# Attention with unshifted exponentials, units of 256 queries, three pairs of score banks and an instruction order from a simulation

## The chip, the cores and the metric

The kernel runs on one core of one Trainium2 chip. The metric is the time of one execution on the device, in microseconds (us). Engines are named as in the profile: PE is the matrix engine (PEld its weight loads), ACT the scalar engine, DVE the vector engine, POOL the GpSimd engine, SP the engine that issues the DMAs. "The granted clock" is the profile's record of how much of its full speed PE was allowed, 1.00 being all of it.

For one core a run counts as slow when it is over 1.5% longer than the fastest run of the same kernel on that occasion.

## The reference

Two attention layers without common data, joined along the last axis. Each has 2048 tokens, width 1024 and 32 heads of 32 columns. The inputs are bfloat16.

```python
# A: ordinary attention, all 2048 x 2048 scores of every head
qkv = (x @ wqkv).reshape(B, S, 3, H, Dh) ...
scores = einsum('bhqd,bhkd->bhqk', q, k) * Dh ** (-0.5)
o = einsum('bhqk,bhkd->bhqd', softmax(scores), v)
a = o... @ wo

# B: four segments of 512 tokens, causal within a segment, with a memory M, z
phi = lambda t: where(t > 0, t + 1.0, exp(t))
for s in range(4):
    p = softmax(qs @ ks.T * scale + causal_mask)
    a_dot = p @ vs
    a_mem = (phi(qs) @ M) / (phi(qs) @ z + 1e-06)
    outs.append(g * a_mem + (1.0 - g) * a_dot)      # g = sigmoid(beta), per head
    M = M + phi(ks).T @ vs
    z = z + phi(ks).sum()
b = concat(outs) @ wo
return concatenate([a, b], axis=-1)
```

The work that can't be avoided is the exponentials of the scores: 134 million in A, and about 21 million in B with some padding. They all go through ACT.

## The kernel before

A Python builder makes the program. It records operations one after the other, keeps a rough clock for each engine, and at each step of PE's clock picks what PE does next: scores first, then the product of probabilities and values (PV), then projections. What comes out is a fixed queue of instructions for each engine, with semaphores between the queues. The order of each queue is fixed when the program is built.

Work comes in units of four heads and 512 queries: 32 of A (16 tiles of 128 keys) and 32 of B, taken in turn. Of the eight PSUM banks that the program uses, two pairs hold scores, two single banks serve the projections and all other side work, one holds the PV sums and one the softmax denominators.

The scores of two heads go into one pair of banks, and one exponential of 128x1024 takes them out. It subtracts a shift, which it reads as one number per partition (`bias=cb`):

```python
SLOTS = [(0, 1), (2, 3)]
PROJ = [4, 5]
OB, LB = 6, 7
# ... emit_scores: n = 2 heads at a time, one bank for each
        for part in range(npart):
            for bk, (st, h) in zip(banks, todo):
                # ...
                    mms.append((self.ps[:, bk, off:off + w], lhsT, rhs))     # 32 rows x 512 queries
        # ...
        cb = (self.cbA if u.kind == "A" else self.cbB)[b][:, 0:1]
        op = R.op("ACT", lambda e: e.activation(self.PT[:, s0:s0 + n, 0:width], self.ps[:, banks[0]:banks[0] + n, 0:width],
                                                ACTF.Exp, bias=cb, scale=SCALE),
                  r=[("ps", bk) for bk in banks[:n]] + [("cb" + u.kind, b)], w=[("PT", s0 + i) for i in range(n)], ...)
```

The shift is an upper bound of the scores, from the largest norms of keys and queries. Each unit of B makes its own, and each group of heads of A. It is a serial chain over four engines:

```python
# b_prep, after the projections of keys and queries of this unit
        for k in range(2):
            R.op("DVE", ... tensor_tensor(self.SQB[k], KQ[:, k, :], KQ[:, k, :], ALU.mult))       # squares
        R.op("PE", ... matmul(self.ps[32 * r:32 * r + 32, bank, :], self.blk32, self.SQB[r % 2]))  # sums per head
        op = R.op("DVE", ... tensor_reduce(self.cbB[b][:, 1:2], self.ps[:, bank, :], AX.X, ALU.max))
        R.op("POOL", ... partition_all_reduce(self.cbB[b][:, 1:2], ..., bass_isa.ReduceOp.max))
        R.op("POOL", ... tensor_scalar(self.cbB[b][:, 0:1], self.cbB[b][:, 1:2], -SCALE, None, ALU.mult))
```

The denominators come out of PE repeated over 32 partitions, and all 128x512 of them go through DVE's reciprocal, in four pieces:

```python
# finish
        for q in range(4):
            cs = slice(128 * q, 128 * q + 128)
            R.op("DVE", lambda e, cs=cs: e.reciprocal(Ls[:, cs], Ls[:, cs]), ..., cost=0.9)
```

The input x of both layers is transposed on the way in by DMA: eight transposes of 128 columns by 2048 rows for A, with B's first unit and its loads issued ahead of them. Projections are full matmuls of 128x128 against 512 columns; V is projected with x as the weights.

## Time and profile before

Two executions took 1605.93 and 1631.54 us, median 1618.74. The profile is of an execution with a span of 1628.9 us.

| | before |
|---|---|
| PE busy | 1393.8 us, 86% |
| ACT busy | 1239.1 us, 76% |
| DVE busy | 792.3 us, 49% |
| mean granted clock | 0.905 |

These lines are from the page of the kernel before: busy time, share of the span and number of instructions of each engine, two lines of the table of 40 slices (busy tenths, and granted clock in tenths), and three groups (busy us in all, mean ns of one, then the idle time of the engine just before them and what ended it).

```profile
span 1628.9 us, 26663 instructions
...
PE 1393.8 (86%) x11550; PEld 466.4 (29%) x11696; DVE 792.3 (49%) x1196; ACT 1239.1 (76%) x1250; POOL 151.8 (9%) x344
...
ACT  0228999698789973969769996478888995598970
...
PEclk9997999798589999979669999688989999998999
...
L392 ACT ACTIVATE PT<-ps,cbA 128x1024 bf16<-128x1024 f32 x1024 | 1050.0, 1197 | 112.9 <-PE ps L380 112.1
L380 PE MATMUL ps<-QA,KA 32*128 32x512 bf16 x2048 | 421.6, 410 | 40.3 <-ACT PT L392 15.3
...
L464 DVE RECIPROCAL Ls<-Ls 128x128 f32<-128x128 f32 x256 | 242.2, 946 | 3.6
```

No engine is full over the whole span. ACT is at nine or ten tenths in some slices and at three to seven in others, and the clock sags in most of the same places.

The waits of the kernel before (who waited for whom: us in all, times, longest):

```profile
ACT PT L392 <- PE ps L380: 145.8, 136, 30.6
ACT PT L392 <- POOL cbB L615: 87.8, 12, 14.2
ACT E L631 <- DVE KQB L508: 55.0, 6, 18.3
...
POOL cbB L615 <- issue: 225.1, 32, 7.6
```

ACT waits for scores, for the shift of B's units, and for B's projections. The last line is inside POOL: after each of the 32 all-reduces of B the next POOL instruction starts about 7 us later (225.1 / 32), though the record of the all-reduce itself is only 0.38 us long. So each shift takes at least 7 us on POOL alone.

The table by stretches (busy us of each engine with the number of instructions, then granted clock, DMA share, GB/s):

```profile
0.00:110.00 110.00, 53.41 (x399) 24.78 (x404) 31.12 (x59) 8.26 (x10) 8.97 (x29) 0.97 0.47 106
110.00:1579.00 1469.00, 1297.74 (x10963) 423.96 (x11098) 739.14 (x1105) 1230.80 (x1240) 142.85 (x315) 0.90 0.11 27
1579.00:1629.00 50.00, 42.62 (x194) 17.61 (x196) 22.04 (x32) 0.00 (x0) 0.00 (x0) 1.00 0.19 69
...
410.00:420.00 10.00, 10.00 (x68) 3.04 (x66) 4.55 (x6) 7.23 (x8) 0.00 (x0) 0.50 0.00 0
```

The fourth number in each row after the length is ACT. Subtracting it from the length gives ACT's idle time: 102 us at the start, 238 in the middle, 50 at the end. The last row is in one of the bouts at half clock: PE busy for all of 10 us, and ACT, which waits for it, for 7.23.

The timeline of the kernel before (start, length, what, how many in a row without a gap), first of ACT, then two lines of PE:

```profile
67.62 2.91 ACT L392 ACTIVATE PT<-ps,cbB 128x1024 bf16<-128x1024 f32 x3 [14.22 <-POOL cbB L615]
...
230.34 31.41 ACT L392 ACTIVATE PT<-ps,cbA 128x1024 bf16<-128x1024 f32 x31
261.37 0.90 ACT L631 ACTIVATE E<-KQB 128x512 bf16<-128x512 bf16 x1
...
413.84 1.11 ACT L392 ACTIVATE PT<-ps,cbA 128x1024 bf16<-128x1024 f32 x1 [0.40 <-PE ps L380]
415.36 1.11 ACT L392 ACTIVATE PT<-ps,cbA 128x1024 bf16<-128x1024 f32 x1 [0.40 <-PE ps L380]
...
1570.61 0.39 PE L380 MATMUL ps<-QA,KA 32*128 32x512 bf16 x2
1570.93 0.40 PE L444 MATMUL ps<-PT,VA 128*32 128x512 bf16 x4
1571.15 0.39 PE L444 MATMUL ps<-PT,ones 128*32 128x512 bf16 x4
```

The first exponential is at 67.62 us, after a wait for the shift. Where nothing disturbs ACT, 31 exponentials start between 230.34 and 261.37 us, so the pitch, start to start, is 1.001 us; at half clock it is 1.52 us (415.36 - 413.84), because PE then takes as long to deliver scores. One visit to the scores, two matmuls of 32 rows by 512 columns, holds PE for 0.32 us (1570.93 - 1570.61). Without a change of tiling, a round of 512 columns takes 0.22 us (1571.15 - 1570.93, four matmuls side by side).

### The profile page before, as it was taken

What the parts mean: (1) busy time and instruction counts of PE and PEld (TensorE: products, weight loads), DVE (VectorE), ACT (ScalarE), POOL (GpSimd) and SP (SyncE); (2) the same over time, 40 slices, a digit from 0 to 9 for tenths busy, and PEclk for the clock granted to TensorE, in tenths of its full rate; (3) what the DMA queues carried; (4) which work ended last, traced back from release to release, by engine and by line L of the source; (5) the groups of instructions that cost most, each with busy time, mean ns of one, the idle gap of its engine ahead of it and who ended that gap; (6) DMA issues with size and microseconds to landing.
All of it is one profiled execution on the core that took longest, in us unless ns stands there. A gap on an engine that the chain in (4) does not pass through costs nothing.

```text
span 1628.9 us, 26663 instructions
## 1 busy us (share of the span) xinstructions
PE 1393.8 (86%) x11550; PEld 466.4 (29%) x11696; DVE 792.3 (49%) x1196; ACT 1239.1 (76%) x1250; POOL 151.8 (9%) x344
## 2 busy tenths in 40 slices
PE   1588999698999987969889998879898997789998
PEld 0241233223223233322223323222332232222223
DVE  0343444353255654645526754545545745463643
ACT  0228999698789973969769996478888995598970
POOL 0000001001011010100101100100101101110100
PEclk9997999798589999979669999688989999998999
DMA  8220001002011001100111101100111001310002
GB/s 167 84 47 7 14 22 39 21 14 46 14 33 27 20 21 46 27 14 21 40 27 28 26 21 27 40 13 20 30 37 33 21 1 27 97 27 7 20 30 75
DMA packets 166742, 54.17 MB, mean 33 GB/s; under 512 B 160480, under 2 KB 160480, under 8 KB 166624
## 3 DMA queue, kind: packets, MB, share of 16 engines
q1 hardware_dynamic: 166624, 52.45, 13.2%
q8 instruction: 92, 1.51, 0.4%
q14 instruction: 26, 0.21, 0.0%
HBM read 35.65 MB, written 8.39 MB: 27 GB/s over the span
## 4 chain that ended last, share of the span: by engine, by line
ACT 57%; PE 23%; issue 8%; DVE 6%; SPq 3%; DMA 2%; POOL 1%; POOLq 0%; ACTq 0%; DVEq 0%
ACT PT L392 56%; PE ps L380 6%; PE ps L444 6%; PE ps L505 5%; PE ps L710 4%; PE ps L522 3%; DVE Ls L464 2%; SPq L293 1%; SPq L306 1%; DMA beta<-in_B_beta_dram 1%; DVE outsb L717 1%; DVE Ls L454 1%; DMA out_dram<-outsb 1%; ACT E L631 1%; DVE cbB L610 1%
## 5 line engine op out<-in xcount | busy, mean ns | idle before, releaser
L392 ACT ACTIVATE PT<-ps,cbA 128x1024 bf16<-128x1024 f32 x1024 | 1050.0, 1197 | 112.9 <-PE ps L380 112.1
L380 PE MATMUL ps<-QA,KA 32*128 32x512 bf16 x2048 | 421.6, 410 | 40.3 <-ACT PT L392 15.3
L392 ACT ACTIVATE PT<-ps,cbB 128x768 bf16<-128x768 f32 (+1 forms) x192 | 175.3, 1039 | 121.7 <-POOL cbB L615 87.8
L444 PE MATMUL ps<-PT,ones 128*32 128x512 bf16 (+3 forms) x2560 | 256.0, 395 | 0.0
L464 DVE RECIPROCAL Ls<-Ls 128x128 f32<-128x128 f32 x256 | 242.2, 946 | 3.6
L380 PEld LDWEIGHTS ps<-QA,KA 32*128 32x128 bf16 x2048 | 96.9, 92 | 462.7 <-ACT PT L392 399.0
L444 PE MATMUL ps<-PT,VA 128*32 128x512 bf16 x2048 | 216.4, 413 | 0.9 <-DVE Os L455 0.4
L505 PE MATMUL ps<-xB,WB 128*128 128x512 bf16 x472 | 147.7, 417 | 53.6 <-DMA xB<-in_B_x_dram 18.2
L505 PE MATMUL ps<-xA,WA 128*128 128x512 bf16 x459 | 141.7, 405 | 29.5 <-DMA xA<-in_A_x_dram 18.9
L415 POOL TENSOR_SCALAR_AFFINE_SELECT PT<-PT 128x256 bf16<-128x256 bf16 (+1 forms) x192 | 95.2, 498 | 472.1 <-ACT PT L392 469.2
L380 PE MATMUL ps<-KQB 32*128 32x128 bf16 (+3 forms) x512 | 65.9, 335 | 50.6 <-ACT PT L392 48.2
L454 DVE COPY Ls<-ps 128x512 f32<-128x512 f32 x64 | 44.0, 687 | 107.4 <-PE ps L444 106.8
L508 DVE CAST KQB<-ps 128x512 bf16<-128x512 f32 x64 | 43.6, 681 | 102.1 <-PE ps L505 102.1
L527 DVE CAST VA<-ps 128x512 bf16<-128x512 f32 x32 | 21.8, 682 | 146.5 <-PE ps L522 146.5
L657 DVE RECIPROCAL den<-den 128x128 f32<-128x128 f32 x96 | 91.3, 951 | 2.5
L444 PEld LDWEIGHTS ps<-PT,VA 128*32 128x32 bf16 x2048 | 53.0, 93 | 129.5 <-issue 120.8
L717 DVE CAST outsb<-ps 128x512 bf16<-128x512 f32 x64 | 43.5, 685 | 84.1 <-PE ps L710 72.0
L522 PE MATMUL ps<-WA,xA 128*128 128x128 bf16 x1024 | 82.5, 231 | 0.8 <-DVE VA L527 0.8
L522 PE MATMUL ps<-WB,xB 128*128 128x128 bf16 x1024 | 79.1, 230 | 1.7 <-DVE KA L508 0.5
L444 PE MATMUL ps<-PT,VB 128*32 128x256 bf16 (+3 forms) x512 | 45.9, 356 | 35.6 <-POOL PT L415 34.6
L710 PE MATMUL ps<-WoB,OTB 128*128 128x512 bf16 x237 | 68.3, 403 | 7.8 <-DVE PKt L678 2.6
L505 PEld LDWEIGHTS ps<-xB,WB 128*128 128x128 bf16 x512 | 40.8, 101 | 107.8 <-issue 67.2
(70 smaller groups left out, 900.1 us busy)
## 6 DMA issues: line engine op xcount, KB each, us to landing
WB<-in_B_wk_dram SPq DMA_DIRECT2D x32, 256.0 KB, 2.9
WB<-in_B_wq_dram SPq DMA_DIRECT2D x32, 256.0 KB, 2.9
WB<-in_B_wv_dram SPq DMA_DIRECT2D x32, 256.0 KB, 2.9
out_dram<-outsb SPq DMA_DIRECT2D x32, 256.0 KB, 2.0
WA<-in_A_wqkv_dram SPq DMA_DIRECT2D x24, 256.0 KB, 2.9
WoB<-in_B_wo_dram SPq DMA_DIRECT2D x1, 2048.0 KB, 17.6
xA<-in_A_wo_dram SPq DMA_DIRECT2D x1, 2048.0 KB, 9.5
xB<-in_B_x_dram SPq DMA_TRANSPOSE x32, 2.8
```

The costliest lines, as they stand in the source:

```text
L380: ins = e.matmul(o, l, r, start=True, stop=True)
L392: op = R.op("ACT", lambda e: e.activation(self.PT[:, s0:s0 + n, 0:width], self.ps[:, banks[0]:banks[0] + n, 0:width], ACTF.Exp, bias=cb, s ...
L415: mo = R.op("POOL", lambda e, ap=ap, pat=pat: e.affine_select(ap, ap, pattern=pat, compare_op=ALU.is_ge, fill=0.0, base=0, channel_multipl ...
L444: ins = e.matmul(o, l, r, start=(st == 0), stop=stop)
L454: R.op("DVE", lambda e: e.tensor_copy(self.Ls2[x][:, :], self.ps[:, LB, :]), r=[("ps", LB)], w=[("Ls", x)], cost=0.66)
L464: R.op("DVE", lambda e, cs=cs: e.reciprocal(Ls[:, cs], Ls[:, cs]), r=[("Ls", x)], w=[("Ls", x)], cost=0.9)
L505: ins = e.matmul(self.ps[:, bank, :], W[:, i, :], xsl(i), start=(i == 0), stop=(i == NI - 1))
L508: op = R.op("DVE", lambda e: e.tensor_copy(dst, self.ps[:, bank, :]), r=[("ps", bank)], w=[dkey], cost=0.66)
L522: ins = e.matmul(self.ps[:, bank, P * t:P * t + P], xsl(i, t), W[:, i, :], start=(i == 0), stop=(i == NI - 1))
L657: R.op("DVE", lambda e, cs=cs: e.reciprocal(self.den[:, cs], self.den[:, cs]), r=["den"], w=["den"], cost=0.9)
L710: ins = e.matmul(self.ps[:, bank, :], lhsT, rhs, start=(j == 0), stop=(j == NG - 1))
L717: op = R.op("DVE", lambda e, ns=ns, bank=bank, ob=ob: e.tensor_copy(self.outsb[ob][:, ns], self.ps[:, bank, :]), r=[("ps", bank)], w=[("ou ...
```

## The change

Nearly the whole kernel is rewritten. The intent, in seven parts:

1. The exponentials lose the shift, and with it the chain that made it. A row of exponentials that leaves the range of numbers would show in its denominator, so all reciprocals are kept and compared with 2^-60 and 2^60 at the end; a flag goes through a branch, behind which lies a complete second program that computes everything with a shift. On these inputs it should never run.
2. Units have 256 queries. Sums and denominators of PV then fit into one bank.
3. Three pairs of banks hold scores. PE fills two pairs in one visit (eight matmuls of 32 rows by 256 columns), and two exponentials empty them.
4. The denominators are transposed in blocks of 32, inverted as 128x8, and spread out again by a transpose.
5. All matmuls but the scores and a few transposes are cut into four column tiles of 32, as PV is. The intent is that PE changes its tiling only around scores.
6. The first 512 rows of x are loaded plainly and transposed by PE, and A goes first.
7. The order of each queue comes from an event simulation in the builder: each engine takes the waiting request of the lowest priority number whose inputs are ready, with modelled durations. The result is again a fixed queue.

The core of the diff, with many cuts:

```diff
-SLOTS = [(0, 1), (2, 3)]
-PROJ = [4, 5]
-OB, LB = 6, 7
+PAIRS = [(0, 1), (2, 3), (4, 5)]
+OB, SB = 6, 7
+ROW, COL, FULL = "row", "col", "full"
+N256, N512 = 0.2235, 0.2175
@@ scores and exponentials
-                                                ACTF.Exp, bias=cb, scale=SCALE),
+        yield do("ACT", lambda e: e.activation(ap, self.ps[:, pr[0]:pr[1] + 1, :], ACTF.Exp, scale=SCALE),
+                 r=[("ps", bk) for bk in pr], w=keys, cost=0.95, prio=0)
+        prs = yield acq(self.pairs, npair)                     # npair = 2
+            for t, q0, w, col in parts:                         # two tiles of keys
+                for h in range(4):
+                    mms.append((prs[h // 2][h % 2], col, t, q0, w, h))
+            yield do("PE", lambda e: f(e, mms), r=keys, w=w, cost=2 * N256, prio=0, mode=ROW)
@@ finish
-            R.op("DVE", lambda e, cs=cs: e.reciprocal(Ls[:, cs], Ls[:, cs]), ...)
+        yield do("DVE", lambda e: e.transpose(Dt[:, :], den), ...)
+        yield do("DVE", lambda e: e.reciprocal(Rc, Dt[:, 0:QU:32]), ...)
+        yield do("DVE", lambda e: e.transpose(Rb..., self.spread(Rc)), ...)
@@ projections
-                    ins = e.matmul(self.ps[:, bank, :], W[:, i, :], xsl(i), start=(i == 0), stop=(i == NI - 1))
+            for c in range(4):
+                ins = e.matmul(self.ps[32 * c:32 * c + 32, bank, :], W[:, i, 32 * c:32 * c + 32], x(i), ...)
@@ order
+    def jprio(self, due):                                       # projections and side work
+        return 10 + (due - self.pos)
+    def pvprio(self):
+        return 5 if len(self.slots.items) < 6 else 14
@@ shift
-        R.op("POOL", lambda e: e.partition_all_reduce(self.cbB[b][:, 1:2], self.cbB[b][:, 1:2], P, bass_isa.ReduceOp.max), ...)
@@ end of every engine's queue
+                self.R.after(eng, self.flagop)
+                v = eng.value_load(self.flag[0:1, 0:1])
+                with eng.If(v != 0):
+                    ...
+                    self.R2.play(eng, name)                     # the shifted program
```

## The prediction

> **What bounds the kernel now.** The page gives ACT 1239.1 us busy of 1628.9 (76%), of which exponentials are 1225 us. In the table of 10 us windows ACT shows 10.00 wherever nothing stalls, and there the timeline shows 19 exponentials of 128x1024 in 19.33 us, a pitch of 1.017 us. So the body is ACT-bound when undisturbed. The other 390 us of ACT idle are: the start (by 110 us only about 8 us of ACT work is done; the first exponential is at 67.6 us, waiting for the shift of POOL L615); the tail (last exponential ends at 1578.6, then 50 us of output projection); and about 240 us between, in bouts at unit boundaries. The waits view puts 87.8 us on the shift and 145.8 us on scores. In those bouts the window table shows a granted clock of 0.50 for 10 to 60 us (400-450, 800-840 us); there PE is 97-100% busy and the pitch of exponentials is 1.51 us. [...]
>
> **What changes.**
> 1. Exponentials lose the per-partition bias. [...]this trace has 1.11 us for an isolated biased 1024 exponential and 0.63 us for an unbiased 512 one. Estimate of the new pitch: 0.93-0.95. Count 1216 -> 1184 (5 instead of 6 per B unit, all 1024 wide). 1184 x 0.94 = 1113, plus 30 for the other ACT work and about 10 of copies: ACT 1150 (about -90).
> 2. The shift disappears: squares, their matmuls, maxima and POOL all-reduces (about 90 us of DVE, 33 of PE) and above all its serial wait.
> 3. The reciprocals of 128x128 (242 + 91 us of DVE) become transposes and 8-wide reciprocals: DVE 792 -> about 500.
> 4. A third score pair gives slack; one bank is left for side work, one for PV, held through a DVE chain of about 1.8 us per unit.
> 5. All other matmuls become column-tiled, so the mode changes only around scores. A change costs about 0.11 us ([...]the next start is 0.32 later). Estimate from rounds of 0.218-0.23 (512) and 0.12 (256): scores and PV 0.88-1.1 us per two exponentials, x512 = 450-560; 256 side jobs x 8 x 0.22 = 450; B and memory 100. PE 1000-1110, 87-97% of ACT. Instructions of PE nearly double (about 46,000).
> 6. Start: x by PE transposes of four row blocks instead of 19 us of queue before the first A projection; first exponential near 15-20 us. Tail about 15-20 us, with flag and branch some 3 us. The shifted program should not run.
>
> **Prediction.** ACT 1150 + start 25 + tail 20 + about 45 us (4%) of stalls: PE and ACT are both near full, and the fixed order comes from modelled costs. 1240 us, range 1180 to 1320. Faster by over 2% 0.96, within 2% 0.02, slower 0.02.
>
> **What would show each step.** Mean exponential about 1.02, saturated pitch 0.93-0.95; ACT busy 1130-1170, over 90% of the span; first exponential before 25 us; last within 25 us of the end; granted clock at least 0.95; no reciprocal of 128x128; DVE under 550.
>
> **What would make it wrong.** PE bound after all: score matmuls of one row group not overlapping with loads, or the doubled instruction stream limiting issue; then PE stays near 97% with exponentials at 1.05 us or more (over 1300). The single side bank or PV bank serialising. [...]Faster than said: if start and stalls stay under 40 us together (1180).

Four passages are cut where marked. In step 1 the pitch of 0.93 to 0.95 us, on which ACT's 1150 us rest, stands as the estimate. The trace of the kernel before allows about the same: an activation of 1024 columns took 1.056 us alone without the operand (L631, from another kind of tile) and 1.114 us with it (L392). The difference of 0.058 us, taken from a pitch of 0.997 to 1.017, gives 0.94 to 0.96 (an estimate). In step 5, for the 0.11 us at a change of tiling, the same trace has rounds of 512 columns of 0.216 to 0.226 us before one of the same tiling and of 0.31 to 0.32 before one of another, so about 0.1.

## The result

Two executions took 1253.77 and 1256.36 us, median 1255.07, against 1618.74 before. The ratio is 0.779, with a 95% interval of 0.769 to 0.790. Such a ratio, here and below, is from fast runs of the same rounds. In the experiments it leaves out the profiled executions, which the times in the table include, so it is not quite the ratio of those times.

The same lines of the page of the kernel after (ACT's exponentials are now L826, scores L809):

```profile
span 1254.4 us, 49504 instructions
...
PE 1081.2 (86%) x23137; PEld 508.4 (41%) x23137; DVE 482.2 (38%) x1065; ACT 1128.8 (90%) x1227; POOL 125.8 (10%) x285
...
ACT  4469999999999899999999889999987999999981
...
PEclk9798999999999999998999999999999999989999
...
L826 ACT ACTIVATE PT<-ps 128x1024 bf16<-128x1024 f32 x1168 | 1086.9, 1067 | 73.0 <-PE ps L809 70.6
...
L809 PE MATMUL ps<-QA,KA 32*128 32x256 bf16 x4096 | 205.8, 275 | 33.0 <-ACT PT L826 26.1
```

ACT is now near full from the fourth slice on. PE works 313 us less, though it runs twice the instructions; of that, the matmuls of A's scores alone give 216 us (421.6 - 205.8). No reciprocal of 128x128 is left.

The waits of ACT in the kernel after:

```profile
ACT PT L826 <- PE ps L809: 70.6, 48, 6.3
...
ACT gcol L483 <- DMA beta<-in_B_beta_dram: 6.3, 1, 6.3
```

The wait for scores has halved, and the shift is gone from the list. The last line is a wait for the small input beta, which will matter at the start.

The stretches of the kernel after, with the same columns as above:

```profile
0.00:100.00 100.00, 67.63 (x1216) 31.34 (x1216) 20.02 (x42) 55.23 (x61) 6.52 (x20) 0.93 0.49 100
100.00:1150.00 1050.00, 916.83 (x19872) 430.07 (x19872) 433.30 (x967) 1001.38 (x1088) 119.29 (x265) 0.98 0.23 50
1150.00:1200.00 50.00, 49.53 (x1104) 24.01 (x1104) 14.88 (x30) 49.43 (x54) 0.00 (x0) 1.00 0.12 40
1200.00:1254.00 54.00, 47.20 (x953) 23.02 (x945) 14.01 (x28) 22.78 (x27) 0.00 (x0) 0.96 0.17 57
```

The timeline of the kernel after, ACT, then PE around one visit to the scores:

```profile
21.93 7.44 ACT L826 ACTIVATE WoB<-ps 128x1024 bf16<-128x1024 f32 x8 [9.44 <-PE ps L809]
29.17 7.53 ACT L826 ACTIVATE OTA<-ps 128x1024 bf16<-128x1024 f32 x8
...
503.20 9.49 ACT L826 ACTIVATE PT<-ps 128x1024 bf16<-128x1024 f32 x10
...
1218.80 3.79 ACT L826 ACTIVATE PT<-ps 128x1024 bf16<-128x1024 f32 x4 [1.56 <-PE ps L809]
...
501.86 0.40 PE L809 MATMUL ps<-QA,KA 32*128 32x256 bf16 x8
502.19 0.40 PE L565 MATMUL ps<-xA,WA 128*32 128x512 bf16 x4
```

The first exponential is at 21.93 us (its output borrows the space of a weight, hence the name WoB), the pitch of the first eight is 0.905 us ((29.17 - 21.93) / 8), and the last exponential ends at 1222.6 us. Over all exponentials that follow one another without a gap, the median from start to start is 0.997 us in the kernel before and 0.904 in the kernel after. A visit to the scores still holds PE for 0.33 us (502.19 - 501.86), but it now feeds two exponentials.

So the 1628.9 us of the one profile become 1254.4 us of the other as follows. Idle time is the length of a stretch less ACT's busy time in it.

| ACT | before | after | difference |
|---|---|---|---|
| busy | 1239 | 1129 | -110 |
| idle at the start (to 110 / 100 us) | 102 | 45 | -57 |
| idle in the middle | 238 | 49 | -189 |
| idle at the end (from 1579 / 1150 us) | 50 | 32 | -18 |
| span | 1629 | 1254 | -374 |

This table says where ACT's time went, not which part of the change did it. One caution: the profile of before is at the slow end of that kernel's own spread. Over 25 runs its time followed its mean clock closely, from 1585 us at 0.946 to 1670 us at 0.878, and the profiled run had 0.905. Against the fast runs of before (means of 1595, 1604 and 1603 us in the three sets of experiments) the gain is 340 to 349 us. The other 25 to 35 us of the table are this slower run of the kernel before; by its lower clock they should lie in the middle row.

### The profile page after: what moved, and what is told of

Read it like the earlier page. It is cut to its first block, busy times and chain, and to the rows that moved or that the text cites. A ratio compares the mean times of both kernels' runs of the same rounds, so it can differ in the third digit from the quotient of the medians.

```text
span 1254.4 us, 49504 instructions
## 1 busy us (share of the span) xinstructions
PE 1081.2 (86%) x23137; PEld 508.4 (41%) x23137; DVE 482.2 (38%) x1065; ACT 1128.8 (90%) x1227; POOL 125.8 (10%) x285
## 4 chain that ended last, share of the span: by engine, by line
ACT 43%; PE 37%; DVE 13%; DMA 2%; issue 2%; SPq 1%; POOL 1%; ACTq 0%
ACT PT L826 42%; PE ps L565 12%; PE ps L897 11%; PE ps L965 7%; PE ps L809 6%; DVE Dt L919 2%; DVE Rb L922 2%; ACT E L670 1%; DVE VT L571 1%; DVE KQB L571 1%; DVE Rall L920 1%; POOL PT L835 1%; DMA beta<-in_B_beta_dram 1%; DVE OTA L926 1%; DVE amem L706 1%
## 5 line engine op out<-in xcount | busy, mean ns | idle before, releaser
L826 ACT ACTIVATE PT<-ps 128x1024 bf16<-128x1024 f32 x1168 | 1086.9, 1067 | 73.0 <-PE ps L809 70.6
L897 PE MATMUL ps<-PT,ones 128*32 128x256 bf16 (+1 forms) x4800 | 298.6, 273 | 0.0
L897 PE MATMUL ps<-PT,VA 128*32 128x256 bf16 x4032 | 256.3, 278 | 33.2 <-ACT PT L826 18.4
L565 PE MATMUL ps<-xA,WA 128*32 128x512 bf16 x3072 | 228.3, 389 | 29.0 <-DVE KQB L571 11.8
L565 PE MATMUL ps<-xB,WB 128*32 128x512 bf16 x3072 | 231.1, 387 | 25.4 <-DVE VT L571 6.7
L809 PE MATMUL ps<-QA,KA 32*128 32x256 bf16 x4096 | 205.8, 275 | 33.0 <-ACT PT L826 26.1
L809 PEld LDWEIGHTS ps<-QA,KA 32*128 32x128 bf16 x4096 | 60.9, 92 | 214.5 <-ACT PT L826 172.1
L897 PEld LDWEIGHTS ps<-PT,ones 128*32 128x32 bf16 x4800 | 130.2, 97 | 15.3 <-issue 0.5
L565 PEld LDWEIGHTS ps<-xA,WA 128*32 128x32 bf16 x3072 | 75.5, 97 | 102.6 <-issue 48.6
L565 PEld LDWEIGHTS ps<-xB,WB 128*32 128x32 bf16 x3072 | 77.0, 97 | 94.0 <-issue 70.3
L965 PE MATMUL ps<-WoB,OTB 128*32 128x512 bf16 x1024 | 72.3, 381 | 5.0 <-DVE VT L571 1.9
L809 PE MATMUL ps<-KQB 32*128 32x128 bf16 (+3 forms) x512 | 44.4, 310 | 5.2 <-ACT PT L826 4.0
```

The costliest lines, as they stand in the source:

```text
L565: ins = e.matmul(self.ps[32 * c:32 * c + 32, bank, :], W[:, i, 32 * c:32 * c + 32], x(i), start=(i == 0), stop=(i == NI - 1))
L809: ins = e.matmul(self.ps[:, bk, col:col + w], lhs(t, hs), rhs(q0, w, hs), start=True, stop=True)
L826: yield do("ACT", lambda e: e.activation(ap, self.ps[:, pr[0]:pr[1] + 1, :], ACTF.Exp, scale=SCALE), r=[("ps", bk) for bk in pr], w=keys, ...
L897: ins = e.matmul(out, l, r, start=st, stop=sp)
L965: ins = e.matmul(self.ps[32 * c:32 * c + 32, bank, :], lhs(j)[:, 32 * c:32 * c + 32], W(j), start=(j == 0), stop=(j == NG - 1))
```

## The experiments

Twelve kernels ran, in three sets, each set on one chip together with runs of the kernel before. All gave correct results. In the table, "time" is the mean of the fast runs, and all runs of the edited kernels were fast. The record calls all twelve comparisons with before "unclear" and doesn't say why; the readings below rest on the intervals, none of which holds 1.

The kernel after was not run again in these sets. Differences from it compare with its own two runs, made on another occasion. Two edits that leave its order alone, a_2rows and a_nobranch, came within 3 us of it, so a difference of a few us from it is not read as an effect.

| kernel | base and edit | time, us | ratio to before (95%) |
|---|---|---|---|
| b_noptr | before, no shift operand | 1547.0 | 0.973 (0.963 to 0.982) |
| b_noshift | before, no shift at all | 1367.2 | 0.857 (0.847 to 0.867) |
| a_ptr | after, with a zero operand | 1339.1 | 0.841 (0.833 to 0.849) |
| a_full_same | after, full projections | 1285.4 | 0.807 (0.800 to 0.814) |
| a_beta | after, real latency of a small DMA in its model | 1252.9 | 0.782 (0.771 to 0.792) |
| a_score | after, real duration of scores in its model | 1369.1 | 0.854 (0.842 to 0.865) |
| a_2pairs | after, two score pairs | 1753.1 | 1.093 (1.067 to 1.119) |
| a_best | after, another order | 1199.1 | 0.748 (0.738 to 0.759) |
| a_2rows | after, scores in another sequence | 1257.4 | 0.784 (0.779 to 0.790) |
| a_nobranch | after, no flag and branch | 1254.0 | 0.783 (0.778 to 0.788) |
| a_thr | after, one number of a priority | 1225.7 | 0.765 (0.760 to 0.771) |
| a_dmax | after, x by DMA alone | 1264.0 | 0.789 (0.783 to 0.795) |

For the later ones, "the replay" that some expectations name is a small program that plays the five fixed queues with durations read from the trace; it gave 1262 us for the kernel after, which took 1255. It served to choose candidates. Only runs on the chip count below.

The main theory was: the gain comes from the exponential's operand and the shift's chain, and the rest from fewer visits of PE to the scores. A rival was that the new order, or the third pair, does it, and that the operand hardly matters.

### The operand alone, on the kernel before: b_noptr

The shift is still computed and still waited for. Only the exponential no longer reads it.

```diff
-                                                ACTF.Exp, bias=cb, scale=SCALE),
+                                                ACTF.Exp, scale=SCALE),
```

> The kernel before with one operand taken away: the exponentials read no per-partition shift (the shift is still computed, and each exponential still waits for it). Theory ACT-bound: the saturated pitch falls from 1.017 us to the 0.949 us seen in the changed kernel; ACT was saturated in about 930 us of the span, so 40 to 65 us less than 1618 us. Rival, PE-bound: in the saturated stretches PE was 93 to 97% busy too, so less than 20 us.

It took 1547.0 us against 1594.8 for before on the same chip: 48 us less, as expected for an ACT-bound kernel. ACT's busy time is 1143.5 us, 96 less than in the profile before. By the difference, about half of what ACT was relieved of came back as idle time. The waits themselves can't be subtracted, as the profile before is of a slow execution, but they stay: 130.3 us for scores and 96.3 for the shift.

### The whole shift away, on the kernel before: b_noshift

```diff
-                                                ACTF.Exp, bias=cb, scale=SCALE),
-                  r=[("ps", bk) for bk in banks[:n]] + [("cb" + u.kind, b)], ...
+                                                ACTF.Exp, scale=SCALE),
+                  r=[("ps", bk) for bk in banks[:n]], ...
@@ a_prep and b_prep: 38 lines deleted
-            R.op("DVE", ... tensor_tensor(...ALU.mult))           # squares
-            R.op("PE", ... matmul(... self.blk32 ...))             # their sums
-            R.op("DVE", ... tensor_reduce(... ALU.max))
-        R.op("POOL", ... partition_all_reduce(...))
-        R.op("POOL", ... tensor_scalar(...))
```

> The kernel before without the shift altogether: no pointer operand, no squares, no maxima, no all-reduce, no wait for them. Theory that the bouts at unit boundaries come from the serial shift chain: the 87.8 us of waits on it and most of the half-clock bouts go too, 150 to 250 us less than before in all, granted clock above 0.95. Rival, that the bouts come from the reciprocals on DVE or from the single bank of PV sums: only 60 to 100 us less, clock still about 0.90.

It took 1367.2 us, 180 less than without the operand alone. This one removal, with the operand, is 228 of the 340 us that lie between the fast runs of before and the kernel after. The expectation held: 150 to 250 us, and a clock above 0.95 (it rose from 0.937 to 0.975). These are ACT's waits, first in b_noptr, then in b_noshift:

```profile
ACT PT L392 <- PE ps L380: 130.3, 114, 30.6
ACT PT L392 <- POOL cbB L615: 96.3, 12, 14.4
ACT E L631 <- DVE KQB L508: 55.7, 6, 18.3
...
ACT PT L392 <- PE ps L380: 95.1, 91, 23.2
...
ACT E L593 <- DVE KQB L508: 22.1, 6, 5.2
```

They fell by 96 us for the shift, 35 for scores and 34 for B's projections, 165 in all, which is the whole difference between the two profiles (1534.6 and 1369.6 us). Work went too: DVE is busy 72 us less, POOL 29 and PE 63, of which the shift's own matmuls are 32. So the waits suggest that the chain's place cost more than its work, but no run keeps the work and drops only the wait. And with the chain gone the old builder arranges PE's other work in another order, so the 180 us hold an effect of order whose size is not known.

What bounds it now shows in its stretches:

```profile
0.00:100.00 100.00, 52.26 (x426) 24.70 (x426) 23.82 (x41) 14.58 (x18) 6.79 (x22) 1.00 0.55 119
100.00:1320.00 1220.00, 1189.37 (x10880) 402.46 (x10879) 669.67 (x947) 1127.32 (x1233) 115.97 (x234) 0.97 0.13 32
```

In the middle PE is busy for 97% of the time (1189.37 of 1220) and ACT for 92%. From here on to the kernel after, PE has to be relieved. In the kernel after the middle has PE at 87% and ACT at 95%. The start is still slow too: ACT has done 14.6 us of work by 100 us, against 55.2 in the kernel after.

### The operand given back to the kernel after: a_ptr

A column of zeros is passed as the bias. The order of all queues is as in the kernel after.

```diff
-        yield do("ACT", lambda e: e.activation(ap, ..., ACTF.Exp, scale=SCALE),
-                 r=[("ps", bk) for bk in pr], w=keys, cost=0.95, prio=0)
+        yield do("ACT", lambda e: e.activation(ap, ..., ACTF.Exp, bias=self.zc[:, 0:1], scale=SCALE),
+                 r=[("ps", bk) for bk in pr] + ["zc"], w=keys, cost=0.95, prio=0)
```

> The changed kernel with a per-partition bias operand given back to the exponentials (a column of zeros written once at the start); every engine's order is unchanged. Theory ACT-bound: 0.068 us on 1184 exponentials is 80 us, of which 60 to 80 us shows, so 1315 to 1335 us. Rival, PE-bound or order-bound: under 30 us.

It took 1339.1 us, 84 more than the kernel after, a little above the range expected. ACT's busy time rises from 1128.8 to 1225.3 us, by 96 us, and its timeline shows the old pitch again:

```profile
500.71 29.37 ACT L826 ACTIVATE PT<-ps,zc 128x1024 bf16<-128x1024 f32 x29
529.76 1.27 ACT L670 ACTIVATE E<-KQB 128x1024 bf16<-128x1024 bf16 x1
```

That is (529.76 - 500.71) / 29 = 1.002 us from start to start; the median over the whole run is 0.997, as in the kernel before, against 0.904. So the operand costs 0.093 us where exponentials follow one another. The expectation was too low because its 0.068 us came from single stretches divided by their count, and the ten exponentials taken from the kernel after hold one step of 1.20 us among steps of 0.90 to 0.92.

In both kernels the operand is 96 us of ACT's busy time. It is worth 48 us of time in the kernel before and 84 in the kernel after, because in one ACT often waits for something else, and in the other it seldom does.

### Column tiles or full matmuls for the projections: a_full_same

```diff
-            for c in range(4):
-                ins = e.matmul(self.ps[32 * c:32 * c + 32, bank, :], W[:, i, 32 * c:32 * c + 32], x(i),
-                               start=(i == 0), stop=(i == NI - 1))
-            return ins
+            return e.matmul(self.ps[:, bank, :], W[:, i, :], x(i), start=(i == 0), stop=(i == NI - 1))
```

The output projections are edited in the same way. The model's costs are left alone, so the order doesn't change.

> The changed kernel with projections and output projections as one matmul on the whole array in place of four column tiles, all orders the same. Theory of mode changes: the array changes mode between side work and the PV sums too, about 0.1 us each, some 1000 or more more changes, which eats the roughly 10% of slack of PE: 20 to 100 us slower. Rival, that PE is limited by its instruction stream (46,000 instructions): 12,000 fewer instructions make it 10 us or more faster.

It took 1285.4 us, 30 more, with 6144 matmuls fewer, as the theory of mode changes expected. Its page:

```profile
PE 1123.9 (88%) x16993; PEld 455.9 (36%) x16993; DVE 482.8 (38%) x1065; ACT 1142.1 (89%) x1227; POOL 126.7 (10%) x285
```

PE is 43 us busier with fewer instructions. So the number of instructions was not what limits PE, and part 5 of the change is worth its price. The case puts a size to a change of the tiling mode: by the timeline of the kernel before, a round of 512 columns takes 0.22 us within a mode, and 0.32 us where the next instruction is of another mode, so about 0.1 us is lost at a change. By the records of PE's matmuls, the mode changes 1235 times in the kernel after and 1989 times here; 754 more at 0.1 us would be some 75 us (an estimate), and PE's busy time rose by 43. Slower matmuls are not the reason: full ones of 512 columns follow each other every 0.216 us in the kernel before, no slower than the 0.22 of a round of column tiles.

### Two score pairs: a_2pairs

```diff
-PAIRS = [(0, 1), (2, 3), (4, 5)]
+PAIRS = [(0, 1), (2, 3)]
```

> The changed kernel with two bank pairs for scores, the third left unused. A batch of scores takes two pairs at once, so with two it can't start before both exponentials have read theirs: after the second, a score group of about 0.4 us and two semaphores stand before the next exponential, 0.5 to 0.6 us on 512 batches. 250 to 350 us slower than 1255, and less clock. Rival, PE or ACT saturated anyway: under 100 us.

It took 1753.1 us: 498 more, and 9% slower than the kernel before. The direction was as expected, the size was far above it. Its waits and its timeline show why. First ACT's wait for scores:

```profile
ACT PT L826 <- PE ps L809: 529.0, 551, 3.3
```

And two lines of its timeline, ACT alone:

```profile
807.38 1.94 ACT L826 ACTIVATE PT<-ps 128x1024 bf16<-128x1024 f32 x2 [0.67 <-PE ps L809]
809.82 1.94 ACT L826 ACTIVATE PT<-ps 128x1024 bf16<-128x1024 f32 x2 [0.50 <-PE ps L809]
```

A visit of PE fills two pairs. With only two, PE can't start the next visit until ACT has emptied both, and ACT then waits out the whole visit, some 0.5 us or more at every second exponential (551 waits, 529 us). That is 0.96 us for each wait, more than the visit: in places PE does other work first (one wait of 3.00 us stands behind 32 projection matmuls), and the mean clock is 0.822. The simulation also knows the number of pairs, so the order is another one, and the 498 us are not the third pair's alone. A visit of one pair was not tried. But the third pair isn't slack on top, as the prediction had it. It lets ACT work while PE makes the large visit, and the large visit is what halves PE's cost of scores for each exponential: 0.32 us before, 0.33 / 2 = 0.165 after. An estimate of the saving from these is 1184 x 0.155 = 184 us of PE; between b_noshift (1285.2) and the kernel after (1081.2) PE's busy time falls by 204 us. The estimate counts only the change of mode on the way out of a visit. There is one on the way in as well, and PE goes to the scores 1158 times in the kernel before and 617 times in the kernel after.

### Another sequence of the score matmuls: a_2rows

In a visit, the two tiles of keys of heads 0 and 1 come first, then those of heads 2 and 3. Each head has its own 32 rows of PE.

```diff
-            for t, q0, w, col in parts:
-                for h in range(4):
-                    mms.append((prs[h // 2][h % 2], col, t, q0, w, h))
+            for pr_ in range(2):
+                for t, q0, w, col in parts:
+                    for h in (2 * pr_, 2 * pr_ + 1):
+                        mms.append((prs[h // 2][h % 2], col, t, q0, w, h))
```

> The changed kernel with the 8 score matmuls of a batch in another sequence: two heads first, then the other two, so two row groups of the array work at a time and not four. All counts, waits and orders of groups are the same. Theory that four row groups run side by side: a group then takes about 0.54 us to the next mode instead of 0.33, 0.21 us on 512 batches is 108 us more of PE, and with PE at 86% some of it shows: 20 to 110 us slower. Rival, that the four row groups are served in turn anyway: within 5 us.

It took 1257.4 us, which is the kernel after. The expectation failed: the group of eight still holds PE for 0.33 us, as its timeline shows (503.10 - 502.77).

```profile
502.77 0.40 PE L810 MATMUL ps<-QA,KA 32*128 32x256 bf16 x8 [0.59 <-ACT PT L827]
503.10 0.61 PE L565 MATMUL ps<-xB,WB 128*32 128x512 bf16 x8
```

The sequence within a visit doesn't matter. But this does not mean, as the rival has it, that the heads are served in turn: the edit left them side by side. By the single records, which the view above merges, the first four matmuls of a visit start within 10 ns of each other in the kernel after and within 17 ns here, and the next four from 120 ns on in both. One after another, at the 0.11 us that a round of 256 columns takes in PV, eight would need some 0.9 us (an estimate), and the visit is over in 0.33. What is also measured is that eight of 256 columns over four heads cost a visit no more than two of 512 over two heads.

### The order: a_score, a_thr, a_best, a_beta

These four change only the order in which the same operations stand in the queues.

a_score: the model charges a visit to the scores 0.447 us plus 0.1 for the mode. The trace says 0.33 in all, so here the model is corrected.

```diff
-            yield do("PE", lambda e: f(e, mms), r=keys, w=w, cost=2 * N256, prio=0, mode=ROW)
+            yield do("PE", lambda e: f(e, mms), r=keys, w=w, cost=N256, prio=0, mode=ROW)
```

> The changed kernel with the model's cost of a score group set right: the trace has 0.33 us from the start of 8 score matmuls to the next mode, about 0.22 plus a change of mode, while the model says 0.447 plus 0.1. All operations and their counts are the same, only the order that the greedy simulation finds is another. A replay of the resulting order with the trace's durations gives 1320 us against 1262 for the order as changed. So if the order alone is worth tens of us: 40 to 70 us slower. Rival, that the engines' queues and semaphores make up for the order: within 15 us.

It took 1369.1 us, 114 more than the kernel after, where 40 to 70 were expected. ACT's waits for scores rise from 70.6 us:

```profile
ACT PT L826 <- PE ps L809: 157.2, 79, 13.3
```

The mean clock falls to 0.928. A truer duration of one kind of operation made a worse order. Why the wrong one does better is not shown; a margin ahead of the scores would be one explanation.

a_thr: PV has a high priority when few slots for probabilities are free. The threshold is lowered.

```diff
-        return 5 if len(self.slots.items) < 6 else 14
+        return 5 if len(self.slots.items) < 2 else 14
```

> The changed kernel with one number of its simulation changed: PV sums go ahead of side work only where fewer than 2 of the 10 slot pairs are free, not fewer than 6. Same operations. Replay of the order with the trace's durations: 1239 against 1262. Theory that side work let go late (projections that scores then wait for) makes the dips: 10 to 35 us faster than 1255. Rival: within 5 us.

It took 1225.7 us, 29 less than the kernel after, for one number and as expected.

a_beta: the four tiny loads of beta are charged 0.1 us each for issue and 2.0 us to land. In the trace they take 0.45 us to issue and 4.9 to 9.8 us to land, and ACT stands still for 6.3 us before the first use. Here the model is told 0.5 and 12.

```diff
-            yield do("SP", f, w=[("beta", h)], cost=0.1, prio=8)
+            yield do("SP", f, w=[("beta", h)], cost=0.5, prio=8, tail=12.0)
```

> The changed kernel with one number of its model changed: the gate values (beta) take 12 us to land in place of 2 (the trace shows about 11). The order of PE and of the DMA queue stays the same; on ACT and DVE the few gate operations move to later. In the trace ACT waits 6.3 us and DVE 14.8 us for beta at 38 to 51 us, the PE bank behind it stays full and the clock falls to 0.67-0.72. Theory that this wait makes the poor start: 8 to 25 us faster than 1255. Rival, that the start waits for x and the first projections anyway: within 4 us.

It took 1252.9 us, so 2 us less, within what the rival allowed. ACT has done 62.7 us of work by 100 us, where it had 55.2, so the start gained 7 us; by 1150 us the lead is down to 5 (1061.8 against 1056.6 us of work done), and the profiled spans differ by 5 too (1254.4 and 1249.1 us). PE's order is unchanged. Where the rest of the lead goes is not shown, and the 2 us between the mean times are less than the runs of one kernel differ among themselves.

a_best: constants of the builder chosen together by the replay, with the last two groups of heads of A interleaved, so that output projections start sooner.

```diff
-        return 10 + (due - self.pos)
+        return 4 + (due - self.pos)
-        return 5 if len(self.slots.items) < 6 else 14
+        return 2 if len(self.slots.items) < 2 else 18
-        span = 66
+        span = 52
-            ... cost=2 * N256, prio=0, mode=ROW)
+            ... cost=1.8 * N256, prio=0, mode=ROW)
-        self.b_rate = 0.56
-        self.ahead = 12
+        self.b_rate = 0.575
+        self.ahead = 28
+        last = [(6, q) for q in range(5)]
+        for q in range(NQ - 5):
+            last += [(7, q), (6, 5 + q)]
+        last += [(7, q) for q in range(NQ - 5, NQ)]
```

The edit of a_beta is in it too, and one limit is clamped so that the builder ends.

> The changed kernel in an order found by a search over the constants of its own simulation (score cost 1.8 x, look-ahead 28, thresholds of priority, rate of B units 0.575), the beta latency set right, and the last two head groups of A interleaved so that their output projection spreads out. Same operations. The replay with the trace's durations gives 1202 us against 1262 for the order as changed (measured 1255). If start, dips and tail are losses of order: 1185 to 1220 us. Rival, that they are dependencies no order removes: within 15 us of 1255.

It took 1199.1 us, within the range expected: 56 us, or 4.5%, less than the kernel after, and a quarter less than before. Its stretches:

```profile
0.00:100.00 100.00, 75.31 (x1492) 36.65 (x1495) 25.23 (x53) 65.68 (x72) 6.58 (x20) 0.95 0.55 105
100.00:1150.00 1050.00, 958.47 (x20908) 450.63 (x20900) 448.64 (x988) 1029.78 (x1121) 119.77 (x265) 0.98 0.24 52
1150.00:1195.00 45.00, 35.19 (x749) 17.32 (x745) 11.54 (x29) 27.98 (x32) 0.00 (x0) 0.97 0.13 42
```

Against the kernel after, ACT's idle time is 34 instead of 45 us at the start, 20 instead of 49 in the middle and 17 instead of 32 at the end. With the same operations, but for four output casts that a_best moves from ACT to DVE, orders from this one builder range from 1199 to 1369 us. The slowest, a_score, is no faster than b_noshift (1367.2 us), the kernel before without its shift. So what the kernel after gains beyond that hangs on its order as much as on its other parts.

### The start and the end: a_dmax and a_nobranch

a_dmax: all of x comes by DMA transposes, and PE's transposes of the first 512 rows go.

```diff
-        yield ("ev", "x0")
-        for c in range(1, 4):
+        for c in range(4):
@@
-        Q.spawn(self.first_x())
```

> The changed kernel with the first 512 rows of x transposed on their way in by the DMA queue, as the other three blocks are, not by PE. One such block takes 5.4 us of the queue in the trace, and the weights are ahead of it. Replay: 1263 against 1262. If the PE transposes are what makes the early start, as the prediction had it: 5 us or more slower. If it is only that 512 rows suffice for the first scores: within 4 us.

It took 1264.0 us, 9 more than the kernel after, and 7 more than a_2rows in the same set. By its time alone this would bear out the prediction's reason. Its trace doesn't: the first exponential is at 18.10 us, earlier than the 21.93 of the kernel after. PE's transposes are not what brings the start forward. Nor are the DMA transposes of x the loss: four of them hold the queue of SP for 18.77 us, until 21.7, and the three of the kernel after hold it until 22.0. But the order changed with the edit. The second transpose of V now stands ahead of B's loads in that queue and goes out at 34.28 us, so that the first of these loads goes out at 35.52 instead of 29.62, and beta at 44.79 instead of 38.77. ACT waits 13.0 us for beta instead of 6.3, and by 100 us it has done 51.4 us of work instead of 55.2.

a_nobranch: the flag is still computed, but it isn't loaded, and the branch is gone.

```diff
-                self.R.after(eng, self.flagop)
-                v = eng.value_load(self.flag[0:1, 0:1])
-                with eng.If(v != 0):
-                    ...
```

> The changed kernel without the load of the flag and the branch at the end, on all engines (the range check itself stays, the shifted program is out of the instruction stream). The trace has the flag ready at 1241.7 us, before the last output matmuls, so only the load and the jump are exposed: 0 to 4 us faster than 1255.

It took 1254.0 us on average over 1246 to 1263, so no difference can be seen. The branch costs at most a few us.

## Why the prediction was right

The prediction was 1240 us in a range of 1180 to 1320. The time was 1255. Term by term:

| term | predicted | measured |
|---|---|---|
| ACT busy | 1150 | 1129 |
| idle at the start | 25 | 45 |
| idle at the end | 20 | 32 |
| stalls between | 45 | 49 |
| sum | 1240 | 1254 |

So the sum is closer than its parts: ACT was put 21 us too high, and start and end together 32 us too low. That these nearly cancel is luck, and so is part of the 45 us of stalls: the prediction could not tell which order the simulation would find, and orders alone move this kernel from 1199 to 1369 us.

- **What bounds it.** "The body is ACT-bound when undisturbed", with 390 us of idle time in three places. Right as a reading. b_noshift adds that with the shift gone the kernel before would have been bound by PE (97% in its middle), so ACT alone was not the limit of the old design.
- **Step 1, the operand.** The mechanism was right. A pitch of 0.93 to 0.95 was predicted, as length over count of a stretch; ten exponentials after 503.20 us give 0.949, but from start to start the median is 0.904. By a_ptr the operand costs 0.093 us (0.997 - 0.904), more than the estimate had allowed for it (1.017 less 0.93 to 0.95 is 0.067 to 0.087). That is one reason why ACT's busy time fell just below the range of 1130 to 1170, and its share is 90.0%, at the edge of "over 90%". The mean recorded length was 1067 ns, not about 1020.
- **Step 2, the shift.** Right that "above all its serial wait" counts. b_noshift shows 180 us for it, more than the 87.8 us that the waits view put down to it; waits for scores and for B's projections fell with it, and the clock rose.
- **Step 3, reciprocals.** DVE fell to 482 us (predicted about 500). What it was worth in time was not tested. DVE was at 52% in b_noshift with all reciprocals in place.
- **Step 4, the third pair.** The DVE chain that holds the PV bank was put at 1.8 us for each unit; from its first transpose to the product that frees the bank it took 1.62 us in A and 1.69 in B (medians). The step itself was too weak. "Slack" was really what lets the large visit overlap with ACT's work: 498 us in a_2pairs, its changed order included.
- **Step 5, tiling.** PE was predicted at 1000 to 1110 us and took 1081, and the loss of about 0.1 us at a change of mode held in the trace and in a_full_same (30 us).
- **Step 6, start and tail.** This is where it failed. The first exponential came at 21.9, not "near 15-20 us". Idle time at the start was counted up to that point alone, but the trace has a second dip of ACT from 44 to 80 us: the wait for beta, then B's first projections. The reason given, PE's transposes, is wrong by a_dmax. The tail was put at 15 to 20 us and a few more; output projections were still queued when the last exponential ended, and they took until some 32 us later, outside the 25 that were said.
- **Step 6, the branch.** Some 3 us were predicted, and no difference was resolved.
- **The clock.** At least 0.95 was predicted, 0.979 measured.
- **Order.** The prediction named "the fixed order comes from modelled costs" only as a reason for stalls of 4%. Experiments show it as a lever of its own: the order alone moved this kernel by +114 and by -56 us.

By the runs, the gain is made up as follows, from the fast mean of before in the first set: operand 48 us, the rest of the shift 180, all other parts together 112. The split holds for this order of steps; given back to the kernel after, the operand alone is 84. The 112 are not taken apart fully, and the new order is one of the parts. The two stretches show 41 us of it at the start and 18 at the end, and the rest in the middle, where b_noshift is bound by PE and the kernel after has halved PE's cost of the scores. The size of the units was never changed alone, since the layout of the banks depends on it.

Open, too, is what takes the clock to half and what holds it there. Of the 18 bouts at 0.50 in the kernel before, 14 begin within a gap of PE of 3.7 to 12 us. The other four have no such gap, and of the seven in the kernel after that begin before PE's last matmul only one has (5.6 us). So gaps alone do not explain the falls. What ends a bout is not shown either: they last 3.4 to 58.0 us, one of the two longest from 398.1 to 456.1 us, and from 400 to 450 us PE is 97 to 100% busy in the records at 0.50. Busy in the records need not mean a full array, since the ends of matmuls are modelled there. The slow clock itself is real: a round of 512 columns takes 0.41 us in that bout (420.75 to 424), and 0.22 outside it.

## What to carry to other kernels

Before giving work to another engine or a chain over several engines, ask which unit must wait for the end of the chain: here a bound with at least 7 us of latency in its chain cost 180 us, its work included. An operand, a bank or a visit is worth what the bounding engine sees of it, so the same edit should be measured in the kernel where it will live (48 us in one, 84 in the other), and buffers be counted against the size of a visit, not one by one. Where the program is a fixed order, try other orders with the same work and take the chip's word: a truer cost in the model made it 114 us slower, and one priority number made it 29 us faster.

## What the runs show of single operations

- The exponential of 128x1024: without the operand one that had waited took 1.023 us (at 930.35 us in the kernel after), and the median from start to start is 0.904, so neighbours overlap by about 0.12 us. With the operand it is the same: 1.114 us alone and 0.997 from start to start in the kernel before.
- A change of the tiling mode: about 0.1 us at each, into the row-tiled scores and out of them (0.32 us, where a round of as many columns within a mode takes 0.22, in the kernel before).
- The all-reduce of one column over the partitions on POOL: every one of 32 took 7.0 us on average until the next POOL instruction (225.1 us in all), behind a record of 0.38 us, in the kernel before.
- A DMA of 0.5 KB in single elements: the four loads of beta in the kernel after, issued within 1.6 us, landed one after another, 1.7 to 2.5 us apart, so that they took 4.9 to 9.8 us from issue to landing, the longest as long as a load of 2 MB (9.6 us).
